# Row-sum reciprocals on GpSimd, and the score banks as two tiles, in a fused top-k attention and feed-forward kernel

## The chip, the core and the metric

The kernel runs on one core of a Trainium2 chip. The time is device microseconds of one execution. The engines are called as in the profile: PE (TensorE matmul), PEld (its weight loads), DVE (VectorE), ACT (ScalarE), POOL (GpSimd) and SP (SyncE, which only issues DMAs here). Each engine works through its own queue in order and waits on semaphores for the others.

## The reference

Eight batches of eight heads, 576 tokens, head size 64. Each query keeps its 32 highest scores, takes a softmax over them and sums the values; the result, 4608 rows of 512, goes through a feed-forward block with an ELU of width 2048.

```python
scores = scale * np.matmul(q, k.transpose(0, 1, 3, 2))
kth = np.partition(scores, -top_k, axis=-1)[..., -top_k:-top_k + 1]
scores = np.where(scores >= kth, scores, -1000000000.0)
scores = scores - np.max(scores, axis=-1, keepdims=True)
attn = np.exp(scores)
attn = attn / (np.sum(attn, axis=-1, keepdims=True) + 1e-09)
attn_out = np.matmul(attn, v)
x = attn_out.transpose(0, 2, 1, 3).reshape(B * S, H * D)
h = x @ w_in
g = np.where(h > 0.0, h, np.exp(np.minimum(h, 0.0)) - 1.0)
out = g @ w_out
```

## The kernel before

The work is cut into 144 steps. A step is one tile of 128 queries and a pair of heads, so two rows of scores per partition (row 0 and row 1), each 576 wide. The steps overlap: while step n is in its selection, step n+2 gets its scores, step n-1 its mask and exponentials, and step n-2 its transposes.

`scores` (L289) writes four matmul results (L298) into PSUM: `wide` is one tile of four banks, banks 0 and 1 for the two halves of row 0, banks 2 and 3 for row 1; each half takes 288 of a bank's 512 columns. Two ACT instructions (L306) copy them to SBUF as `sc`. The free columns behind them serve as well: `transpose_qk` (L246) puts the last keys and queries of a head pair through bank 1 (L256, read by ACT at L261), and `turn` (L385) puts the fifth of nine transposed score chunks through bank 3 (L400 with output `scps`, read by ACT at L401). The other chunks go through a pool of their own (L400 with output `eps`), as do the other transposes of keys and queries (L268, read by ACT at L274).

`select` (L332) finds the 32nd highest value with four passes of MAX8 (L339, L351) and three of MATCH_REPLACE8 (L344) on DVE, both rows in turn. `select_row` (L311; L317, L321, L327) does the same in the first eight steps. `mask` (L355) has POOL negate that value and form a difference (L364, L366), and ACT runs Prelu and Exp over the row in place (L367, L368), with the sums of the row in `den`. `normalise` (L372) adds epsilon on POOL (L377), takes the reciprocal on DVE (L379) and scales both rows on POOL (L381). `attend` (L410) multiplies the transposed chunks with the values (L426), and ACT copies the result into `xT` (L453).

The feed-forward block is cut into pieces. `hidden` has 4 matmuls (L484), three ACT instructions (L496 to L498) and later one on DVE (L465); `project` has matmuls (L507), whose results ACT copies (L516) for the store. `feed` slips these pieces between the parts of the steps, by costs and due times fixed in the source. The weights come as raw 64-bit numbers and are decoded during the first eight steps on ACT (L167 to L169), POOL (L170, L184) and DVE (L177, L180).

In these eight steps a scheduler orders the instructions of each engine. From the ninth on (`n == tight`, L657) the four compute engines keep the order of the source. In a step of this kind `mask` of the rows of the step before comes in the first half, and `normalise` after the last selection pass of the current step:

```python
        next(passes)
        if prev:
            normalise(prev)
        feed(n, 0.25)
        turn_qk(True)
```

Of the kernel before, what the change touches and what calls it, by code (L numbers as in the profile page):

```python
# [8 lines left out]
AF = mybir.ActivationFunctionType  # L9
ALU = mybir.AluOpType  # L10
FP32 = mybir.dt.float32
# [69 lines left out]
def kernel(  # L81
# [9 lines left out]
    nc = tc.nc  # L91
    P = nc.NUM_PARTITIONS
# [3 lines left out]
    JP = J * P  # L96
    R = S - JP
    HS = S // 2
# [6 lines left out]
    scale = 1.0 / float(D) ** 0.5  # L105
# [3 lines left out]
    def pool(name, bufs, **kw):  # L109
        return ctx.enter_context(tc.tile_pool(name=name, bufs=bufs, **kw))  # L110

    const = pool("const", 1)
# [8 lines left out]
    ps_sc = pool("ps_sc", 1, space=PSUM)  # L121
    ps_t = pool("ps_t", 2, space=PSUM)
    ps_f = pool("ps_f", 2, space=PSUM)
    wide = ps_sc.tile([P, 4, JP], FP32, tag="s", name="scps")
    late = {}
    raws = ExitStack()
    early = raws.enter_context(tc.tile_pool(name="early", bufs=1))
# [2 lines left out]

    ident = const.tile([P, P], FP32, tag="ident", name="ident")
    make_identity(nc, ident[:])
    w_in = const.tile([P, NC, dff], FP32, tag="w_in", name="w_in")
    w_out = const.tile([P, NF, dm], FP32, tag="w_out", name="w_out")

# [110 lines left out]
    def transpose_qk(b, hp):  # L246

        d = kvpool.tile([P, 4 * J + 3, D], FP32, tag="kqT", name="kqT")
        kqT[b, hp] = d[:].rearrange("p c d -> p (c d)")
        srcs = [loaded.pop((b, hp, name)) for name in ("k", "q")]
        ps = wide[:, 1, HS : HS + 3 * R]
        for i in range(2):
            nc.tensor.transpose(  # L256
                ps[:, i * R : i * R + P],
                srcs[0][:, J, :, :].rearrange("p h d -> p (h d)"),
                ident[:],
            )  # L260
        nc.scalar.copy(  # L261
            d[:, 0 : 4 * J + 3 : 2 * J + 1, :],
            ps.rearrange("p (a s) -> p a s", a=3),
        )
        for i, src in enumerate(srcs):
            ps = ps_t.tile([P, JP], FP32, tag="t", name="qkps")
            for c in range(J):
                nc.tensor.transpose(  # L268
                    ps[:, c * P : (c + 1) * P],
                    src[:, c, :, :].rearrange("p h d -> p (h d)"),  # L270
                    ident[:],
                )
            c0 = KEYS + i * (2 * J + 1) * D
            nc.scalar.copy(kqT[b, hp][:, c0 : c0 + JP], ps[:])  # L274
            yield

    def start_qk(b, hp):
        turning.append(transpose_qk(b, hp))
# [10 lines left out]
    def scores(u):  # L289

        u.sc = scpool.tile([P, 2, S], FP32, tag="sc", name="sc")
        q0 = QUERIES + u.t.qt * P
        for half in range(2):
            for h, i, rows in u.heads:
                kq = kqT[u.t.b, h // 2]
                part = slice(i * D, (i + 1) * D)
                k0 = (KEYS if i == 0 else 0) + half * HS
                nc.tensor.matmul(  # L298
                    wide[rows, 2 * i + half, 0:HS],
                    kq[part, q0 : q0 + u.t.ql],  # L300
                    kq[part, k0 : k0 + HS],
                    start=True,
                    stop=True,
                )
        for i in range(2):
            nc.scalar.activation(  # L306
                u.sc[:, i, :].rearrange("p (a s) -> p a s", a=2),
                wide[:, 2 * i : 2 * i + 2, 0:HS], AF.Copy, scale=scale,
            )

    def select_row(u, i):  # L311
# [58 lines left out]
        )  # L370

    def normalise(u):  # L372
        if u.normal:
            return
        u.normal = True
        den = small.tile([P, 2], FP32, tag="dene", name="dene")
        nc.gpsimd.tensor_scalar_add(den[:], u.den[:], EPS)  # L377
        rec = small.tile([P, 2], FP32, tag="rec", name="rec")
        nc.vector.reciprocal(rec[:], den[:])  # L379
        for i in range(2):  # L380
            nc.gpsimd.tensor_scalar(  # L381
                u.sc[:, i, :], u.sc[:, i, :], rec[:, i : i + 1], 1.0, ALU.mult, ALU.mult
            )

    def turn(u, chunks):  # L385

        if u.turned:
            return
        g = u.group
        if g.et is None:  # L390
            g.et = etpool.tile([P, 2 * J + 1, len(g.tiles), P], FP32, tag="et", name="et")
        if chunks.stop - chunks.start == 1:
            ps = wide[:, 3, HS : HS + P]
        else:
            ps = ps_t.tile([P, JP], FP32, tag="t", name="eps")
        sc = u.sc[:, :, :].rearrange("p i s -> p (i s)")
        n = chunks.stop - chunks.start
        for c in range(n):
            c0 = (chunks.start + c) * P
            nc.tensor.transpose(ps[:, c * P : (c + 1) * P], sc[:, c0 : c0 + P], ident[:])  # L400
        nc.scalar.copy(  # L401
            g.et[:, chunks, u.at, :],
            ps[:, 0 : n * P].rearrange("p (c q) -> p c q", c=n),
        )
        if chunks.stop == 2 * J + 1:
            u.turned = True
            if u.at == len(g.tiles) - 1:
                closing.append(g)
# [127 lines left out]
    for b in range(B):  # L536
# [12 lines left out]
        for qt in range(J + 1):  # L549
            r0 = b * S + (JP if qt == J else qt)  # L550
            if qt == J:
                (blk, slot), c0, n = slots[rest], (b % 2) * R, R
                rows = slice(r0, r0 + R)
            else:
                (blk, slot), c0, n = slots[(b % 2) * J + qt], 0, P
                rows = slice(r0, r0 + J * (P - 1) + 1, J)
# [26 lines left out]
    for b in range(1, B):  # L583
        f = first[b]
# [30 lines left out]
    start_qk(0, 0)  # L615
    turn_qk(True)
    scores(steps[0])
    load_qk(0, 2)
    start_qk(0, 1)
    turn_qk(True)  # L620
    scores(steps[1])
    load_qk(0, 3)
    for hp in range(1, NHP):
# [10 lines left out]
    for n in range(NS + 3):  # L634
# [3 lines left out]
        if n < tight:  # L638
            turn_qk(True)
            scores(ahead)  # L640
            for i in range(2):
                passes = select_row(cur, i)
                next(passes)
                if i == 0:
                    while closing:
                        attend(closing.pop(0))
                elif prev:
                    normalise(prev)
                    turn(prev, main)
                    turn(prev, rest)  # L650
                    turn(prev, other)
                feed(n, 0.25)
                next(passes)
                mask(cur, i)
                feed(n, 0.25)
            continue
# [27 lines left out]
        if prev:  # L684
            normalise(prev)
# [38 lines left out]
```

## Time and profile before

| | |
|---|---|
| time, median of 3 runs | 1712.81 us (1712.72 to 1713.59) |
| time of the profiled execution | 1713.55 us |
| its span, first to last instruction | 1711.8 us |
| PE, PEld busy | 93%, 60% |
| DVE, ACT, POOL busy | 91%, 69%, 25% |
| mean granted TensorE clock | 0.973 |
| HBM traffic over the span | 32 GB/s |

A line of the profile names the source line, the engine, the operation, and the tiles written and read ("rec<-dene"). "Idle before" is time for which the engine stood still in front of an instruction, with the instruction that ended the wait. Matmuls overlap, and so do instructions that follow each other closely on one engine, so starts are a better measure of an engine's pace than durations. In a timeline the columns are the start, the time and the count of a merged run of equal instructions.

### The profile page before, as it was taken

What the parts mean: (1) busy time and instruction counts of PE and PEld (TensorE: products, weight loads), DVE (VectorE), ACT (ScalarE), POOL (GpSimd) and SP (SyncE); (2) the same over time, 40 slices, a digit from 0 to 9 for tenths busy, and PEclk for the clock granted to TensorE, in tenths of its full rate; (3) what the DMA queues carried; (4) which work ended last, traced back from release to release, by engine and by line L of the source; (5) the groups of instructions that cost most, each with busy time, mean ns of one, the idle gap of its engine ahead of it and who ended that gap; (6) DMA issues with size and microseconds to landing.
All of it is one profiled execution on the core that took longest, in us unless ns stands there. A gap on an engine that the chain in (4) does not pass through costs nothing.

```text
span 1711.8 us, 26507 instructions
## 1 busy us (share of the span) xinstructions
PE 1593.9 (93%) x8560; PEld 1029.6 (60%) x8560; DVE 1551.1 (91%) x3392; ACT 1180.3 (69%) x2813; POOL 432.7 (25%) x1142
## 2 busy tenths in 40 slices
PE   4558999999999999999999999999999999999999
PEld 3345676667575666655557575755557575755565
DVE  7899999999999999999999999999989999998600
ACT  5886786778686776768658585867758686767531
POOL 3664222222222222222222222222222212222100
PEclk8569999999999999999999999999999999999999
DMA  6531021001100111001100111001100000000000
GB/s 168 171 126 54 15 48 35 7 7 43 48 7 7 29 35 41 1 15 41 43 18 1 34 35 35 7 13 40 32 26 7 21 21 28 7 7 7 7 13 13
DMA packets 101130, 56.24 MB, mean 33 GB/s; under 512 B 84096, under 2 KB 92288, under 8 KB 100992
## 3 DMA queue, kind: packets, MB, share of 16 engines
q1 hardware_dynamic: 100992, 54.55, 11.5%
q8 instruction: 68, 1.11, 0.3%
q14 instruction: 70, 0.57, 0.1%
HBM read 45.09 MB, written 9.44 MB: 32 GB/s over the span
## 4 chain that ended last, share of the span: by engine, by line
PE 64%; DVE 23%; ACT 8%; issue 3%; POOL 1%; DMA 1%; SPq 0%; ACTq 0%; POOLq 0%
PE ops L507 25%; PE hps L484 19%; DVE wk L344 8%; PE avps L426 7%; DVE m L351 7%; PE scps L298 6%; PE eps L400 4%; DVE m L339 2%; DVE gT L465 2%; ACT sc L367 2%; ACT sc L368 2%; DVE wk L321 1%; DVE m L327 1%; ACT et L401 1%; ACT n L498 1%
## 5 line engine op out<-in xcount | busy, mean ns | idle before, releaser
L484 PE MATMUL hps<-xT,w_in 128*128 128x256 f32 (+2 forms) x2432 | 555.7, 377 | 24.8 <-ACT gT L497 16.9
L351 DVE MAX8 m<-wk 128x8 f32<-128x576 f32 x816 | 574.9, 745 | 0.0
L507 PE MATMUL ops<-w_out,gT 128*128 128x512 f32 x1152 | 522.6, 598 | 0.0
L484 PEld LDWEIGHTS hps<-xT,w_in 128*128 128x128 f32 x2432 | 410.1, 194 | 126.0 <-ACT gT L497 23.8
L344 DVE MATCH_REPLACE8 wk<-m,wk 128x576 f32<-128x576 f32 x544 | 399.5, 741 | 0.0
L507 PEld LDWEIGHTS ops<-w_out,gT 128*128 128x128 f32 x1152 | 208.6, 190 | 232.8 <-issue 197.5
L381 POOL TENSOR_SCALAR sc<-sc,rec 128x576 f32<-128x576 f32 x288 | 218.8, 769 | 254.7 <-DVE rec L379 234.0
L367 ACT ACTIVATE sc<-sc,neg 128x576 f32<-128x576 f32 x288 | 226.6, 787 | 55.9 <-POOL neg L364 55.6
L377 POOL TENSOR_SCALAR dene<-den 128x2 f32<-128x2 f32 x144 | 34.4, 239 | 879.5 <-ACT sc L368 878.9
L368 ACT ACTIVATE sc<-sc,gap 128x576 f32<-128x576 f32 x288 | 223.2, 775 | 26.3 <-ACT sc L367 1.5
L306 ACT ACTIVATE sc<-scps 128x576 f32<-128x576 f32 x288 | 173.0, 660 | 80.5 <-PE scps L298 80.4
L401 ACT COPY et<-eps 128x512 f32<-128x512 f32 x288 | 167.2, 581 | 74.3 <-PE eps L400 74.2
L426 PE MATMUL avps<-et,vT 128*64 128x256 f32 (+2 forms) x2080 | 190.4, 324 | 14.3 <-ACT et L401 13.7
L400 PE MATMUL eps<-ident,sc 128*128 128x128 f32 x1152 | 177.8, 280 | 24.7 <-POOL sc L381 24.6
L400 PEld LDWEIGHTS eps<-ident,sc 128*128 128x128 f32 x1152 | 145.2, 145 | 92.2 <-issue 48.4
L344 DVE MATCH_REPLACE8 wk<-m,sc 128x576 f32<-128x576 f32 x272 | 199.7, 741 | 0.0
L298 PE MATMUL scps<-kqT 64*128 64x288 f32 (+1 forms) x1280 | 186.5, 440 | 11.1 <-ACT et L401 6.1
L339 DVE MAX8 m<-sc 128x8 f32<-128x576 f32 x272 | 191.2, 744 | 0.0
L496 ACT ACTIVATE n<-hps 128x256 f32<-128x256 f32 (+2 forms) x304 | 112.4, 370 | 91.9 <-PE hps L484 89.0
L465 DVE SCALAR_TENSOR_TENSOR gT<-n,gT 128x256 f32<-128x256 f32 (+2 forms) x304 | 128.9, 430 | 49.6 <-ACT n L498 49.6
L426 PEld LDWEIGHTS avps<-et,vT 128*64 128x64 f32 x2080 | 120.6, 140 | 87.8 <-issue 28.7
L298 PEld LDWEIGHTS scps<-kqT 64*128 64x128 f32 (+1 forms) x1280 | 100.2, 182 | 76.6 <-issue 22.2
(43 smaller groups left out, 1066.1 us busy)
## 6 DMA issues: line engine op xcount, KB each, us to landing
kin<-in_k_dram SPq DMA_DIRECT2D x64, 128.0 KB, 2.8
qin<-in_q_dram SPq DMA_DIRECT2D x64, 128.0 KB, 2.8
raw<-in_moe_w_in_dram SPq DMA_DIRECT2D x16, 512.0 KB, 4.1
vT<-in_v_dram SPq DMA_DIRECT2D x64, 128.0 KB, 2.2
raw<-in_moe_w_out_dram SPq DMA_DIRECT2D x16, 512.0 KB, 3.2
out_dram<-osb SPq DMA_DIRECT2D x32, 256.0 KB, 2.2
kin<-in_k_dram SPq DMA_DIRECT2D x32, 32.0 KB, 2.5
kin<-in_q_dram SPq DMA_DIRECT2D x32, 32.0 KB, 2.3
```

The lines of the kernel that those rows point to most:

```text
L298: nc.tensor.matmul(wide[rows, 2 * i + half, 0:HS], kq[part, q0 : q0 + u.t.ql], kq[part, k0 : k0 + HS], start=True, stop=True,)
L339: nc.vector.max(found[i], cur[i])
L344: nc.vector.match_replace(wk[i], found[i], cur[i], TAKEN)
L351: nc.vector.max(found[i], cur[i])
L367: nc.scalar.activation(sc, sc, AF.Prelu, bias=neg[:], alpha=STEEP)
L368: nc.scalar.activation(sc, sc, AF.Exp, bias=gap[:], accum_out=u.den[:, i : i + 1])
L381: nc.gpsimd.tensor_scalar(u.sc[:, i, :], u.sc[:, i, :], rec[:, i : i + 1], 1.0, ALU.mult, ALU.mult)
L400: nc.tensor.transpose(ps[:, c * P : (c + 1) * P], sc[:, c0 : c0 + P], ident[:])
L401: nc.scalar.copy(g.et[:, chunks, u.at, :], ps[:, 0 : n * P].rearrange("p (c q) -> p c q", c=n),)
L426: nc.tensor.matmul(ps[i * D : (i + 1) * D, cols], vt[:, 2 * J + i if c == J else i * J + c, :], w, start=(c == 0), stop=(c == J),)
L484: nc.tensor.matmul(ps[:, 0:n_tok], w_in[:, i, f * P : (f + 1) * P], blk.xT[:, i, 0:n_tok], start=(i == 0), stop=(i == NC - 1),)
L507: nc.tensor.matmul(blk.o[:], blk.gT[f // NG][:, f % NG, s * P : (s + 1) * P], w_out[:, f, :], start=(f == 0), stop=(f == NF - 1),)
```

## The change

DVE's reciprocal becomes four instructions on POOL: the sum to the power of -1 (with a constant tile `power` as the exponent), and a Newton step r(2 - dr) in three instructions, all on 128 x 2 numbers. The epsilon add before them and the scaling behind them stay on POOL. The constant tile takes one POOL memset at the start. The score tile of four banks becomes two tiles of two banks, one for each row; every use is renamed to the same bank as before, so the columns and the order in the source stay as they were.

```diff
-    wide = ps_sc.tile([P, 4, JP], FP32, tag="s", name="scps")
+    wide = [ps_sc.tile([P, 2, JP], FP32, tag=f"s{i}", name="scps") for i in range(2)]
...
+    power = const.tile([P, 2], FP32, tag="power", name="power")
+    nc.gpsimd.memset(power[:], -1.0)
...
-        ps = wide[:, 1, HS : HS + 3 * R]
+        ps = wide[0][:, 1, HS : HS + 3 * R]
...
-                    wide[rows, 2 * i + half, 0:HS],
+                    wide[i][rows, half, 0:HS],
...
-                wide[:, 2 * i : 2 * i + 2, 0:HS], AF.Copy, scale=scale,
+                wide[i][:, :, 0:HS], AF.Copy, scale=scale,
...
         rec = small.tile([P, 2], FP32, tag="rec", name="rec")
-        nc.vector.reciprocal(rec[:], den[:])
+        nc.gpsimd.tensor_tensor(rec[:], den[:], power[:], ALU.pow)
+        nc.gpsimd.tensor_tensor(den[:], den[:], rec[:], ALU.mult)
+        nc.gpsimd.tensor_scalar(den[:], den[:], -1.0, 2.0, ALU.mult, ALU.add)
+        nc.gpsimd.tensor_tensor(rec[:], rec[:], den[:], ALU.mult)
...
-            ps = wide[:, 3, HS : HS + P]
+            ps = wide[1][:, 1, HS : HS + P]
```

## The prediction, made before the changed kernel ran

> **What bounds the kernel now.** I read the page first (busy shares and the 40 slices), then a table of stages, then the waits of PE and of DVE by stage, and last a timeline of one step.
>
> ```profile
> span 1711.8 us, 26507 instructions
> PE 1593.9 (93%) x8560; PEld 1029.6 (60%) x8560; DVE 1551.1 (91%) x3392; ACT 1180.3 (69%) x2813; POOL 432.7 (25%) x1142
> ```
>
> Two engines are nearly full, so the average says little. The table of stages (busy time of PE, PEld, DVE, ACT, POOL in each stretch, then granted clock, DMA share and GB/s) separates them.
>
> ```profile
> 0.00:150.00 150.00, 83.29 (x457) 62.66 (x459) 127.67 (x249) 112.40 (x251) 85.66 (x130) 0.72 0.49 146
> 150.00:800.00 650.00, 614.63 (x3695) 410.84 (x3691) 643.13 (x1439) 472.20 (x1182) 155.80 (x455) 1.00 0.10 25
> 800.00:1640.00 840.00, 828.23 (x4180) 513.97 (x4177) 773.51 (x1691) 577.60 (x1330) 191.23 (x558) 1.00 0.08 21
> 1640.00:1712.00 72.00, 67.73 (x238) 42.10 (x236) 6.80 (x16) 18.12 (x53) 0.00 (x0) 1.00 0.03 11
> ```
>
> From 150 to 800 us DVE is busy 643.1 of 650 and PE idles 35.4: DVE is the bound. From 800 to 1640 PE is busy 828.2 of 840 and DVE idles 66: PE is the bound, with 11.8 us of holes. After 1640 only PE's feed-forward matmuls are left. The opening holds eight steps and the decoding of the weights.
>
> PE's waits, first from 150 to 800 (two of its rows), then all of 800 to 1640, then DVE's waits for the reciprocal's input in those two stretches (us in total, times, longest):
>
> ```profile
> PE scps L256 <- ACT sc L306: 8.5, 6, 1.9
> PE scps L400 <- ACT kqT L261: 5.4, 6, 1.5
> ```
>
> ```profile
> PE scps L400 <- ACT kqT L261: 8.0, 8, 2.2
> PE scps L256 <- ACT sc L306: 3.2, 2, 1.9
> PE avps L426 <- ACT et L401: 0.2, 1, 0.2
> ```
>
> ```profile
> DVE rec L379 <- POOL dene L377: 6.5, 7, 1.6
> ```
>
> ```profile
> DVE rec L379 <- POOL dene L377: 51.9, 26, 14.3
> ```
>
> Nearly all of PE's holes after 800 stand in front of writes to the score banks. L400 (the fifth transpose, bank 3) waits for L261, which reads bank 1: another bank, so the wait comes from the banks being one tile. The timeline of one step shows the chain of the row sums:
>
> ```profile
> 511.88 0.23 POOL L377 TENSOR_SCALAR dene<-den 128x2 f32<-128x2 f32 x1 [4.51 <-ACT sc L368]
> 514.09 1.41 DVE L351 MAX8 m<-wk 128x8 f32<-128x576 f32 x2
> 515.41 0.15 DVE L379 RECIPROCAL rec<-dene 128x2 f32<-128x2 f32 x1
> 515.48 0.40 DVE L465 SCALAR_TENSOR_TENSOR gT<-n,gT 128x256 f32<-128x256 f32 x1
> 515.73 1.49 POOL L381 TENSOR_SCALAR sc<-sc,rec 128x576 f32<-128x576 f32 x2 [3.62 <-DVE rec L379]
> 516.78 0.57 PEld L400 LDWEIGHTS eps<-ident,sc 128*128 128x128 f32 x4
> 517.19 0.42 POOL L364 TENSOR_SCALAR neg<-m 128x1 f32<-128x1 f32 x1
> 517.64 0.78 ACT L367 ACTIVATE sc<-sc,neg 128x576 f32<-128x576 f32 x1 [1.21 <-POOL neg L364]
> ```
>
> The sum plus epsilon is ready at 512.11. POOL then idles 3.62 us, until DVE has worked off its queue and comes to the reciprocal; POOL scales the rows only then, and the negated threshold of the next rows (L364) stands behind that, with ACT waiting 1.21 us for it.
>
> **Part 1: the reciprocal leaves DVE.** 144 RECIPROCALs, 0.151 us each, are 21.8 us of busy time. But DVE's instructions overlap: here the next one starts 0.07 us after the reciprocal, and without it would start where the reciprocal did. So the queue gains about 0.065 us a step: 62 steps from 150 to 800, 4.0 us. The wait for L377 goes too: 6.5 us there. That is 10.5 us at most where DVE is the bound. PE has 35.4 us of holes in the stretch, so it can follow, but where DVE waited, ACT or PE were late themselves. I take 7. After 800 the 51.9 us of DVE waits are worth nothing by themselves, since PE is busy 98.6%: DVE would only wait elsewhere, for scores. Its instruction order on the long part of the run is otherwise unchanged in the built program.
>
> **Part 2: four instructions more on POOL.** The chain from L377 to L381 becomes power, multiply, multiply-add, multiply, each waiting for the one before. Multiply: 0.19 us (TENSOR_TENSOR L366, 53.7 us over 288). Multiply-add: 0.23 (L377). A hand-over within an engine: about 0.1 us (ACT's L367 to L368). No row shows a power. From below it is the 0.19 of L366; the longest TENSOR_TENSOR that the trace has on POOL, L184's 1.28 us for 512 columns, is the other end. I take 0.5, nearer the lower row because there are only two columns. Chain: 0.5 + 0.19 + 0.23 + 0.19 + five hand-overs of 0.1 = 1.6 us (1.3 to 2.4), in place of a mean 1.6 us that POOL waits for DVE now (234.0 us over 144) and 0.3 for the hand-overs there and back.
>
> What hides it: in the step shown PE takes the scaled rows at 516.78 and one scaling lasts 0.75, so it may begin as late as 516.03, that is 3.9 us after L377's end. Over the steps from the ninth on the same subtraction gives 3.0 at the least, 3.5 for one in twenty, 5.9 in the middle. So up to 3 us this chain costs nothing, and mostly L381 and the neg behind it come earlier, which takes part of ACT's 55.6 us of waiting for neg. Queued behind the chain on POOL are L381, then L364 and L366 of the next rows; ACT's L367 waits for those.
>
> The Trainium skill speaks against the move: GPSIMD Engine Reference, section 4.1 Engine selection, calls GpSimd about twice as slow as VectorE on two-input elementwise work. At one or two columns the rows say 0.187 against 0.151. By the rule the three two-input instructions would take 0.30 each and the chain 1.6 us, still under the cover, so the sum would not change.
>
> **Contention.** L465 reads two SBUF tiles; it usually takes 0.40 us at 256 columns, 0.423 in the mean, once 1.28 (the longest of any form). The excess of that form is 176 x 0.023 = 4.0 us. POOL gets 144 x 1.1 = 160 us busier on 433, so a third more: 1 to 3 us over the run, half of it where DVE binds. It is in the step from 10.5 to 7. The skill's page SBUF — State Buffer, section Who interferes with whom, gives the reason: a DVE instruction with two SBUF inputs fetches the second through the read interface shared with GpSimd. By the rule alone, if each added POOL instruction held up one of DVE's for its whole length, 160 us would go; the row, where 433 us of POOL work cost 4, is far below that.
>
> **Part 3: two score tiles.** In the built program L400's wait for L261 is gone (it now waits for the second eviction L306, which is earlier), L256 waits for the first of the two evictions (one eviction, 0.65 us, sooner), and the first score matmul L298 waits for nothing, with the second taking over the wait for L401. ACT's first eviction starts one matmul sooner. After 800: 8.0 us of L261 waits plus 2 x 0.65 = 9.3; what comes next, the transposes that wait for L274's copy, stands behind four or more matmuls. I take 9. Before 800 the same waits (5.4 us and part of 8.5) lie beside a full DVE and only give PE room.
>
> **Part 4: opening and tail.** The scheduler orders the opening anew on all engines. DVE waits 21.9 us there for POOL's L170, and POOL gets 7 x 1.1 = 8 us more work in a stretch where it is 57% busy; the reciprocals' wait is gone in return. Between -4 and +10; I take +1. The tail is PE's alone: 0.
>
> **Sum.** -7 - 9 + 1 = -15 us. The profiled execution took 1713.55 (span 1711.8 and 1.75 around it), 0.74 above the median of 1712.81: 1698.5 on it, 1698 as a median.
>
> **Rivals.**
> Slower: power is a long software loop. POOL's cycle is neg at 517.19, through ACT's four passes, to the next L377's end at 522.82: 5.6 us, then the chain, then 1.5 of scaling; 7.1 + chain. Steps take 10.8 us (L339 from 144.0 to 1606.0 over 135 steps). From a chain of 3.7 us, a power of about 2.6, POOL is the bound, and each further us costs 136: a power of 3 us gives some 1750, of 4 us some 1890. For: no row has it. Against: two columns only.
> No change: ACT and PE's own lateness holds DVE up elsewhere, PE meets the next wait (L274, gT) after each one removed, and the opening loses 8: -15 becomes -3 to +3, 1710 to 1716. For: both engines are nearly full, so relief on one is soon capped by the other.
> Slower by the opening alone: POOL's added 8 us and the new order land on DVE's L177 in full, and part 1 gives 2, part 3 gives 3: +5, 1718.
> The change does not do what it says: excluded for the waits, which the built program shows; the gain of part 3 could still be a shift.
>
> **The numbers.** 0.2% (3.4 us) is about what a measurement can tell. My forecast 0.64, own range 1685 to 1708 (all of 10.5, 11.8, and 4 to 6 from the opening and earlier ACT work below; 2 + 5 less 2 above). No change 0.12; long power 0.17; opening 0.07. Faster 0.64, same 0.12, slower 0.24. The range 1685 to 1718 leaves out the long power and little else.
>
> **What would show it.** Right: no L379 on DVE and no waits there; L400 no longer waiting for L261; PE over 99% busy from 800; L381 starting 1.3 to 2.4 us after L377's end. Wrong: a power over 2.6 us, ACT waiting longer for neg than 55.6 us, PE's eps waiting for POOL after 150 us, or an opening that ends later (first L339 after 144.0).

## The result, and the profile after

The changed kernel takes 1694.03 us (median of 4 runs, 1692.54 to 1695.23) against 1713.07 (4 runs): ratio 0.9888, 95% interval 0.9877 to 0.9900. That is 19 us faster; 15 had been forecast. The profiled execution has a span of 1693.4 us against 1711.8.

The page of the changed kernel (span; busy time, share and instructions):

```profile
span 1693.4 us, 26805 instructions
PE 1597.5 (94%) x8560; PEld 1035.0 (61%) x8560; DVE 1542.7 (91%) x3248; ACT 1179.6 (70%) x2813; POOL 627.0 (37%) x1719
```

The stages (stretch; PE, PEld, DVE, ACT, POOL busy; clock; DMA; GB/s), the last one now ending at 1694:

```profile
0.00:150.00 150.00, 88.73 (x435) 64.93 (x437) 124.04 (x231) 108.52 (x240) 90.52 (x155) 0.72 0.50 146
150.00:800.00 650.00, 621.97 (x3738) 417.59 (x3737) 649.97 (x1399) 477.75 (x1196) 244.28 (x714) 1.00 0.10 25
800.00:1640.00 840.00, 837.24 (x4225) 521.22 (x4224) 762.77 (x1606) 579.09 (x1337) 292.24 (x851) 1.00 0.08 21
1640.00:1694.00 54.00, 49.52 (x167) 31.23 (x165) 5.96 (x14) 14.29 (x44) 0.00 (x0) 0.99 0.03 10
```

From 150 to 800 us DVE no longer stands still at all (650.0 of 650), and from 800 to 1640 PE's holes shrink from 11.8 to 2.8 us. PE's waits from 800 to 1640 after the change, all of them:

```profile
PE scps L258 <- ACT sc L308: 2.1, 2, 1.3
PE avps L432 <- ACT et L407: 0.2, 1, 0.2
```

The 8.0 us in front of the fifth transpose (now L406) are gone, as the split into two tiles promised. DVE's waits in that stretch are not fewer, they only have another name:

```profile
DVE gT L471 <- ACT n L504: 76.6, 21, 42.9
```

The row-sum chain in one step, by the timeline (start, time):

```profile
500.77 0.23 POOL L380 TENSOR_SCALAR dene<-den 128x2 f32<-128x2 f32 x1 [4.58 <-ACT sc L370]
501.08 0.72 POOL L382 TENSOR_TENSOR rec<-dene,power 128x2 f32<-128x2 f32 x1
501.88 0.21 POOL L383 TENSOR_TENSOR dene<-dene,rec 128x2 f32<-128x2 f32 x1
502.17 0.19 POOL L384 TENSOR_SCALAR dene<-dene 128x2 f32<-128x2 f32 x1
502.45 0.20 POOL L385 TENSOR_TENSOR rec<-rec,dene 128x2 f32<-128x2 f32 x1
502.75 1.48 POOL L387 TENSOR_SCALAR sc<-sc,rec 128x576 f32<-128x576 f32 x2
504.25 0.23 POOL L366 TENSOR_SCALAR neg<-m 128x1 f32<-128x1 f32 x1
```

From the end of L380 (501.00) to the scaling (502.75) it is 1.75 us; over the steps 1.73 in the middle. POOL no longer idles in it. The next rows' neg follows 0.02 us behind the scaling; in this step its input, a MAX8 of L353, was done only 0.07 us before the scaling's end (504.16 against 504.23). How tight this place is, the experiments e5 to e8 ask.

Two of the prediction's own signs of being wrong did come: the opening ends later (the first MAX8 of the ninth step at 150.3 instead of 144.0 us), and ACT's waits for neg are 56.1 us against 55.6, though part of them had been expected to go.

**Where the time went.** PE's order of instructions is the same in both kernels after the opening, so the start of the same matmul in two traces tells how far one is ahead. Negative is earlier than in the kernel before, in us. "Ninth step" is the first MAX8 of the ninth step on DVE (144.0 us before), the others are feed-forward matmuls of L484, the 129th, 1153rd and 2049th of them, which started at 169.0, 760.7 and 1463.3.

| run | ninth step, DVE | PE at 169 | PE at 761 | PE at 1463 | end |
|---|---|---|---|---|---|
| the change | +6.3 | +1.9 | -4.7 | -18.3 | -18.4 |
| e1, tiles only | +1.7 | +1.0 | -4.2 | -18.4 | -18.4 |
| e2, reciprocal only | +6.5 | +0.4 | -5.6 | -5.7 | -5.6 |
| e3, change, DVE reciprocal in the opening | +2.2 | +3.5 | -7.4 | -21.6 | -21.6 |
| e4, change, idle reciprocal on DVE | +5.7 | +1.3 | -3.4 | -17.1 | -17.1 |
| e5, two powers more | +16.5 | +13.3 | +15.6 | +16.0 | +18.5 |
| e6, four powers more | +26.3 | +26.4 | +85.9 | +138.9 | +148.8 |
| e7, no Newton step | +9.3 | +2.4 | -8.7 | -23.0 | -23.0 |
| e8, e7 and idle POOL work | +9.3 | +2.4 | -8.5 | -22.8 | -22.8 |
| e9, a version from these | +2.1 | +3.2 | -8.8 | -23.1 | -23.1 |
| e10, e9 without the Newton step | +2.0 | +3.1 | -7.9 | -22.2 | -22.2 |
| e11, the change again | +6.7 | +2.3 | -5.0 | -18.7 | -18.7 |

So the change lost 1.9 us in the opening as PE sees it, gained 6.6 between 169 and 761, and 13.6 after that. Each row is one execution. The two of the changed kernel agree within 0.4 us, but the executions of one kernel spread over 1 to 4 us, and the profiled one is the slowest of four for the change and the fastest of four for e1; a difference of 1 or 2 us between two rows shows little.

### The profile page after: what moved, and what is told of

Read it like the earlier page. It is cut to its first block, busy times and chain, and to the rows that moved or that the text cites. A ratio compares the mean times of both kernels' runs of the same rounds, so it can differ in the third digit from the quotient of the medians.

```text
span 1693.4 us, 26805 instructions
## 1 busy us (share of the span) xinstructions
PE 1597.5 (94%) x8560; PEld 1035.0 (61%) x8560; DVE 1542.7 (91%) x3248; ACT 1179.6 (70%) x2813; POOL 627.0 (37%) x1719
## 4 chain that ended last, share of the span: by engine, by line
PE 68%; DVE 21%; ACT 5%; issue 2%; POOL 2%; DMA 1%; SPq 0%; ACTq 0%; POOLq 0%; DVEq 0%
PE ops L513 25%; PE hps L490 21%; PE avps L432 8%; DVE wk L346 7%; PE scps L300 7%; DVE m L353 6%; PE eps L406 5%; DVE m L341 2%; DVE gT L471 1%; DVE wk L323 1%; DVE m L329 1%; PE qkps L270 1%; ACT sc L370 1%; ACT sc L369 1%; ACT et L407 1%
## 5 line engine op out<-in xcount | busy, mean ns | idle before, releaser
L353 DVE MAX8 m<-wk 128x8 f32<-128x576 f32 x816 | 574.9, 745 | 0.0
L490 PE MATMUL hps<-xT,w_in 128*128 128x256 f32 (+2 forms) x2432 | 554.3, 376 | 19.3 <-ACT gT L503 19.3
L490 PEld LDWEIGHTS hps<-xT,w_in 128*128 128x128 f32 x2432 | 409.5, 194 | 119.9 <-ACT gT L503 26.4
L380 POOL TENSOR_SCALAR dene<-den 128x2 f32<-128x2 f32 x144 | 34.9, 243 | 819.6 <-ACT sc L370 819.0
L369 ACT ACTIVATE sc<-sc,neg 128x576 f32<-128x576 f32 x288 | 226.5, 787 | 56.6 <-POOL neg L366 56.1
L387 POOL TENSOR_SCALAR sc<-sc,rec 128x576 f32<-128x576 f32 x288 | 218.7, 769 | 15.2 <-POOL rec L385 0.4
L300 PE MATMUL scps<-kqT 64*128 64x288 f32 (+1 forms) x1280 | 198.1, 438 | 21.5 <-ACT sc L308 14.7
L471 DVE SCALAR_TENSOR_TENSOR gT<-n,gT 128x256 f32<-128x256 f32 (+2 forms) x304 | 129.1, 431 | 95.3 <-ACT n L504 95.3
L406 PEld LDWEIGHTS eps<-ident,sc 128*128 128x128 f32 x1152 | 144.5, 145 | 93.4 <-issue 48.9
L406 PE MATMUL eps<-ident,sc 128*128 128x128 f32 x1152 | 177.9, 280 | 21.8 <-POOL sc L387 18.6
L300 PEld LDWEIGHTS scps<-kqT 64*128 64x128 f32 (+1 forms) x1280 | 106.0, 180 | 90.2 <-issue 45.1
```

The costliest lines, as they stand in the source:

```text
L300: nc.tensor.matmul(wide[i][rows, half, 0:HS], kq[part, q0 : q0 + u.t.ql], kq[part, k0 : k0 + HS], start=True, stop=True,)
L353: nc.vector.max(found[i], cur[i])
L369: nc.scalar.activation(sc, sc, AF.Prelu, bias=neg[:], alpha=STEEP)
L387: nc.gpsimd.tensor_scalar(u.sc[:, i, :], u.sc[:, i, :], rec[:, i : i + 1], 1.0, ALU.mult, ALU.mult)
L490: nc.tensor.matmul(ps[:, 0:n_tok], w_in[:, i, f * P : (f + 1) * P], blk.xT[:, i, 0:n_tok], start=(i == 0), stop=(i == NC - 1),)
```

## The experiments

**e1 and e2: each part alone.** e1 makes the two tiles of the change and keeps DVE's reciprocal; e2 does the reverse.

```diff
 e1: + wide = [ps_sc.tile([P, 2, JP], ...) for i in range(2)]   (and its four uses)
       nc.vector.reciprocal(rec[:], den[:])
 e2:   wide = ps_sc.tile([P, 4, JP], ...)
     + power, tensor_tensor(pow), mult, mult-add, mult on nc.gpsimd
```

> Only the two score tiles; the reciprocal stays on DVE. The split theory (both parts pay: the reciprocal where DVE binds, the tiles where PE binds): PE's holes in front of L400 and L256 go after 800 us, -9 to -13 us there, before 800 DVE still waits for the reciprocal's input and little is gained (0 to -3); opening 0; in all about -11, 1702. The tiles-alone theory (PE's instruction order is the clock everywhere, and all of the gain stood in front of the banks): -18 to -24, 1689 to 1695, the whole gain of the change or more.

> Only the reciprocal on GpSimd; one score tile as before. Split theory: -7 between 150 and 800 us, nothing after it, since PE still waits for L261 in front of L400 (some 8 us after 800), and +2 to +6 in the opening; in all -3 to -7, about 1708. Tiles-alone theory: 0 in the long part and the opening's loss, 1713 to 1718.

e1: 1696.74 us, ratio 0.9899 (0.9886 to 0.9913). e2: 1707.90, 0.9967 (0.9954 to 0.9979). The gains, 16.8 and 5.6 us against 1713.53 in the same job, add up to 22.4, and both together give 19. (By the medians alone this difference of 3.4 us is hardly clear of the noise: each of the three gains is good to about 2 us.) Neither theory is right as stated. The tiles pay in both stretches (-5.2 between 169 and 761, -14.2 after), the reciprocal in the first alone (-6.0, then -0.1). Together they give -6.6 in the first stretch, not -11.2. Part of the overlap is seen in the wait of DVE for the sum from 150 to 800 us, which was 6.5 us before; with the tiles alone it is

```profile
DVE rec L379 <- POOL dene L377: 2.6, 4, 0.8
```

Freeing PE fills holes of DVE, and so does letting DVE go on without the sum; it can only be done once. In that stretch DVE stands still for 6.9 us before, 2.6 in e1, 2.6 in e2 and not at all in the change: each part alone takes 4.3, both together 6.9. That is 1.7 of the 4.6 us by which the parts fall short of their sum; where the rest goes isn't shown. After 800 us e2 shows the wait that only the tiles remove still in place:

```profile
PE scps L405 <- ACT kqT L263: 7.7, 6, 2.2
```

On top of the tiles, the reciprocal's move is worth 2 to 3 us by the medians (1696.74 against 1694.03 and, in e11, 1694.72) and nothing by the profiled executions (-18.4 both); the intervals of the ratios overlap.

**e3: the opening.**

```diff
-                    normalise(prev)           # in the steps before the ninth
+                    normalise(prev, True)     # True: nc.vector.reciprocal
```

> The change, but the first eight steps (those that the scheduler orders) keep the reciprocal on DVE. If GpSimd's extra work there is what makes the opening later, the ninth step starts near 144 us again and PE's first feed-forward matmuls are 2 to 3 us earlier: 1688 to 1692. If the opening's loss comes from the new order that the two tiles give, it stays: 1693 to 1695.

1692.36 us, ratio 0.9873 (0.9860 to 0.9887), 2 us below the change by the medians, with intervals that overlap. The ninth step starts at +2.2 instead of +6.3. PE's landmark at 169 us is not earlier (+3.5), but the gain is there at 761 (-7.4 against -4.7). Four of the 6.3 us come from the reciprocal's move, 1.7 from the order that the tiles give (e1). That it is POOL's added work is not shown: e7 below has less of it in the opening (POOL busy 85.4 us up to 150 against 90.5), and its ninth step starts later still (+9.3). The scheduler orders the opening anew in each of these kernels, and that may be all of it.

**e4: the place in DVE's queue.**

```diff
+        idle = small.tile([P, 2], FP32, tag="idle", name="idle")
+        nc.vector.reciprocal(idle[:], power[:])
```

> The change, with a reciprocal of a constant on DVE at the old place in each step, which waits for nothing and which nobody reads. If the reciprocal's place in DVE's queue is what costs where DVE binds (0.065 us a step), +4 between 150 and 800 us: 1697 to 1699. If it is the wait for the sum that cost, or PE alone sets the pace, 0 to +1: 1694 to 1695.

1696.19 us, ratio 0.9898 (0.9883 to 0.9913), 2.2 us over the change's first median. From the ninth to the 71st step on DVE (144.0 to 799.3 us before) the trace goes from +5.7 to -1.7, the change's from +6.3 to -4.9: 3.8 us for 62 steps, 0.06 each, near the 0.065 read from the starts; against e11's trace it is 2.6, 0.04 each. At the end 1.3 of them are left (-17.1 against -18.4). A little issue time on the bound engine is real, and most of it no longer shows where PE binds.

**e5 and e6: is the chain under cover?** Two and four powers more, each waiting for the one before.

```diff
         nc.gpsimd.tensor_tensor(rec[:], den[:], power[:], ALU.pow)
+        for _ in range(2):                     # e6: 4
+            nc.gpsimd.tensor_tensor(rec[:], rec[:], power[:], ALU.pow)
```

> The change with two more powers in the chain (1/x twice, so the value comes back): the time from the sum plus epsilon to the scaling grows from 1.73 to about 3.3 us in every step. Cover theory (PE takes the scaled rows 3 us or more after the sum in every step, 5.9 in the middle): 0 to +4 us, 1694 to 1698, half of it in the opening. Loop theory (POOL, ACT's four passes and POOL again make a cycle of 5.7 + chain + 1.5, against a step of 10.6): the cycle is 10.5, just under the step, so also little, up to +5.

> The change with four more powers: chain about 4.9 us. Loop theory: the cycle is 5.7 + 4.9 + 1.5 = 12.1 against 10.6 a step, so POOL becomes the bound and the steps lengthen by 1.5 each, +150 to +210 us, 1850 to 1900. Cover theory alone (only steps whose scaling comes later than PE needs it pay): a few tens at most, 1700 to 1730.

e5: 1731.65 us, ratio 1.0106 (1.0090 to 1.0123), with a chain of 3.28 us in the middle. e6: 1866.70, 1.0889 (1.0872 to 1.0906), chain 4.81. The cover theory falls: e5 costs 37 us where 0 to 4 were expected, 11 of them in the opening (+13.3 against +1.9 at 169) and the rest along the whole run. Nor is it for want of the scaled rows: PE waits for them (L408) 6.5 us in e5 from 150 to 1640. The loop theory missed e5 too (up to +5), since it took a cycle of 10.5 against a step of 10.6 for room enough. e6 is what it said. The loop can be read from e6's timeline:

```profile
500.72 1.48 POOL L389 TENSOR_SCALAR sc<-sc,rec 128x576 f32<-128x576 f32 x2
...
502.17 0.24 POOL L366 TENSOR_SCALAR neg<-m 128x1 f32<-128x1 f32 x1
...
502.44 0.78 ACT L369 ACTIVATE sc<-sc,neg 128x576 f32<-128x576 f32 x1 [0.65 <-POOL neg L366]
...
506.53 0.23 POOL L380 TENSOR_SCALAR dene<-den 128x2 f32<-128x2 f32 x1 [3.65 <-ACT sc L370]
506.84 0.72 POOL L382 TENSOR_TENSOR rec<-dene,power 128x2 f32<-128x2 f32 x1
507.64 2.99 POOL L384 TENSOR_TENSOR rec<-rec,power 128x2 f32<-128x2 f32 x4
...
511.57 1.48 POOL L389 TENSOR_SCALAR sc<-sc,rec 128x576 f32<-128x576 f32 x2
```

Scaling, neg, ACT's four passes, the sum, the chain, the next scaling: 500.72 to 511.57, 10.85 us with ACT at its quickest (502.17 to 506.76, 4.59). Over the steps ACT's part is 5.3 us in the middle: 5.3 + 4.8 + 1.5 = 11.6, and the steps last 11.6 us up to the 71st and 11.8 after. In e5 the same sum is 5.6 + 3.3 + 1.5 = 10.4, or 11.0 with ACT's 6.2 in the later half, and the steps last 10.5 and 11.1. This agreement is no proof by itself: where neg starts directly behind the scaling (115 of 136 steps in e5 and in e6) the sum comes to about a step, whichever engine binds. That the loop binds is seen in ACT, which takes neg up 0.04 us after its end in the middle of e5 and 0.03 in e6, against 0.81 in the change; its part shrinks from 6.9 us to 5.7 and 5.3. Its waits for neg over the run, first the change, then e5, then e6, say the same:

```profile
ACT sc L369 <- POOL neg L366: 56.1, 46, 3.3
```

```profile
ACT sc L369 <- POOL neg L366: 153.4, 86, 6.5
```

```profile
ACT sc L369 <- POOL neg L366: 326.9, 123, 7.3
```

In the change neg starts directly behind the scaling in 92 of 136 steps (115 before), but ACT mostly has other work when neg is ready, so the loop isn't tight there. What looked like cover is this other work of ACT, which fits into the loop while there is room; the two powers of e5 use the room up.

**e7 and e8: shorter chain, or less work on POOL?** e7 leaves out the Newton step, so its reciprocals have the power's own precision. e8 does too, and puts three idle multiplies of constants where POOL waits for the exponentials.

```diff
 e7: -  nc.gpsimd.tensor_tensor(den[:], den[:], rec[:], ALU.mult)
     -  nc.gpsimd.tensor_scalar(den[:], den[:], -1.0, 2.0, ALU.mult, ALU.add)
     -  nc.gpsimd.tensor_tensor(rec[:], rec[:], den[:], ALU.mult)
 e8: +  if i == 1 and ordered:              # in mask, from the ninth step on
     +      for _ in range(3):
     +          idle = small.tile([P, 2], FP32, tag="idle", name="idle")
     +          nc.gpsimd.tensor_tensor(idle[:], power[:], power[:], ALU.mult)
```

> The change without the Newton step (the power's own precision): three POOL instructions fewer in each step, chain about 0.9 us. If the chain is under cover, nothing in the long part, and 0 to -2 from POOL's lighter opening: 1692 to 1694. If POOL's extra instructions cost DVE or ACT something all along, -3 or more.

> The power alone (no Newton step), and from the ninth step on three POOL multiplies of constants that nobody reads, put where POOL waits for the exponentials, so POOL does the same amount of work as in the changed kernel but the chain stays at 0.9 us. Chain theory (what counts is the time from the sum to the next rows' neg): as without the Newton step, 1690 to 1692. Work theory (POOL's extra instructions hold others up wherever they stand): as the changed kernel, 1693 to 1695.

e7: 1691.42 us, ratio 0.9872 (0.9857 to 0.9887). e8: 1691.32, 0.9871 (0.9857 to 0.9886). A chain of 0.9 instead of 1.73 us gives 3 us, and the same work outside the chain costs nothing: it is not POOL's load that counts. That it is the length of the loop is not shown. The gain comes before 761 us (-8.7 against -4.7), and from the ninth to the 71st step DVE doesn't stand still in either kernel, so what e7 gains there must lie in DVE's own work. In large part it does: from the start of a two-input instruction (L471 in the change) to the start of the next takes 38.5 us in sum in e7 and e8, 41.7 in the change and 42.9 in e11, and most of the difference is time for which POOL's scaling holds these instructions up (1.1 and 1.2 us against 3.7 and 4.9; more on this under contention below). With the shorter chain the scaling falls beside fewer of them; no run separates this from the loop. e11, the changed kernel again in the job of e8, ran at 1694.72, ratio 0.9891 (0.9876 to 0.9906).

> The changed kernel once more, on the same chip as these three, as their measure: 1692 to 1696 by every theory.

**e9 and e10: a better version.** Two tiles, DVE's reciprocal in the first eight steps, GpSimd's after them, and no epsilon add; e10 leaves out the Newton step as well.

```diff
-        nc.gpsimd.tensor_scalar_add(den[:], u.den[:], EPS)
...
+        if early:
+            nc.vector.reciprocal(rec[:], u.den[:])
+        else:
+            nc.gpsimd.tensor_tensor(rec[:], u.den[:], power[:], ALU.pow)
+            ...                                # e9: the Newton step on u.den
```

> A version that the runs point to: two score tiles, DVE's reciprocal in the first eight steps, GpSimd's power and Newton step after them, and no epsilon add (the sum holds exp(0) = 1, beside which 1e-9 vanishes in fp32), so the chain is one instruction shorter, about 1.45 us. By chain theory -1 against the change with DVE's reciprocal in the opening: 1689 to 1692. If the chain is well under cover: 1692.

> The same without the Newton step (the power's own precision): chain about 0.6 us. By chain theory another -2 to -3: 1686 to 1690. If the chain is well under cover: 1692.

e9: 1688.56 us, ratio 0.9857 (0.9843 to 0.9872), 6 us below the change in the same job. e10: 1689.38, 0.9856 (0.9840 to 0.9873). e9 is just below what was expected; e10 lies inside its range of 1686 to 1690, but its further 2 to 3 us below e9 did not come, and the runs of the two overlap. So a chain shorter than about 1.45 us shows no gain in this version. What binds there was not tried; in the trace of e9 PE still waits 14.3 us for ACT's reading of PSUM into gT (L504 there, L497 before) between 150 and 800 us.

## Why the prediction was right, and which steps were wrong

The sign, the size (-15 against -19) and the two places were right. The sum, -7 - 9 + 1, had three terms that were off and partly cancelled; the traces give -6.6, -13.6 and +1.9. That the total came out so near is luck in part: the tiles alone give 16.8 us where 9 had been put on them, and the reciprocal on top of them 2 to 3 where 7 had been.

- **Part 1, 7 us where DVE binds.** Alone it was 6.0 (e2). The step that failed is the sum over the parts, which took them as separate. Part 3 was put at nothing before 800 us, "beside a full DVE". It gave 5.2 there (e1). DVE's waits for the sum were in part PE's lateness handed on: they fall from 6.5 to 2.6 us with the tiles alone. After that only 1.4 of part 1 was left. The reading that DVE's 51.9 us of waits after 800 were worth nothing held: e2 gains 0.1 there.
- **Part 3, 9 us after 800.** The waits named were the right ones, the term was too small: 14.2 alone. Compared start by start, the fifth transpose is 9.8 us earlier in sum, L256 1.1, and matmuls of L484 that follow each other 2.8. The wait table gave 8.0 for the first, probably because the modelled end of a matmul covers the beginning of a wait. The third stands in no wait table: in the kernel before, PE's granted clock was half of full speed for 3.4 us (0.50 from 817.80 to 821.20) right behind two of the longest holes, and the eight matmuls of L484 behind the fifth transpose took 4.29 us there; the same eight take 2.75 in the change, where the hole is gone (before, then change):

  ```profile
  817.89 0.45 PE L400 MATMUL scps<-ident,sc 128*128 128x128 f32 x1 [2.20 <-ACT kqT L261]
  818.13 4.29 PE L484 MATMUL hps<-xT,w_in 128*128 128x384 f32 x8
  ```

  ```profile
  810.33 0.27 PE L406 MATMUL scps<-ident,sc 128*128 128x128 f32 x1
  810.44 2.75 PE L490 MATMUL hps<-xT,w_in 128*128 128x384 f32 x8
  ```

  The other place is at 1183.0 us, behind a wait of 1.86 us at L256 (1.32 in the change, and no such stretch behind it). The 2.2 us of hole in front of 1211.8 are not followed by one. In these traces the clock changes only at the ends of windows of 3.41 us (817.8 and 1183.0 are 107 of them apart); the first two holes lie in one window each, the third is cut in two by an end at 1210.35, which may be why, but no run tests it. In the change and in e1 no such stretch is left between 800 and 1640 us.
- **Part 2, the chain.** 1.6 us forecast, 1.73 measured. The power was taken as 0.5 and is 0.72 us, within the ends of 0.19 and 1.28; a hand-over costs 0.08. The step that failed is "up to 3 us this chain costs nothing". That came from the moment at which PE takes the scaled rows. The nearer deadline was neg, behind the scaling on POOL (e5 and e6). So 3.3 us cost 37 (e5). A chain 0.8 us shorter than the change's gave 3 (e7), but for another reason, at least in part (contention, below). The slower rival had the right mechanism, and its threshold of 3.7 was too high: it set one step's ACT time of 5.6 us against the mean step of 10.8. By e5's ACT times and the change's steps it would be 10.4 - 5.6 - 1.5 = 3.3 up to the 71st step and 10.8 - 6.2 - 1.5 = 3.1 after it. Each further us cost 88 from e5 to e6, not 136, as ACT's part shrank. The change's chain stayed below either threshold.
- **Contention, 1 to 3 us.** DVE's two-input instruction took 128.9 us in all before and 129.1 after, with 194 us more of POOL's busy time: no net cost. But the two engines do collide. A two-input instruction of DVE that begins while a pass of POOL's scaling runs is longer than usual by what the pass has left, less 0.14 us. Here the second pass began at 523.11, had 0.62 us left, and made an instruction of usually 0.40 us one of 0.89:

  ```profile
  522.38 1.48 POOL L387 TENSOR_SCALAR sc<-sc,rec 128x576 f32<-128x576 f32 x2
  523.24 0.89 DVE L471 SCALAR_TENSOR_TENSOR gT<-n,gT 128x256 f32<-128x256 f32 x1
  ```

  That happened 23 times before (4.9 us in sum), 18 times in the change (4.8), 44 in e5 (12.0), 14 in e7 (4.3). The added instructions hold up nothing: 41 of the L471 began beside the row-sum chain, 23 of them during a power, and none was more than 0.06 us longer than usual. So what counts is where POOL's long passes fall, and not how much it does, as the estimate took it.
- **The opening, +1.** +6.3 on DVE and +1.9 on PE: mis-sized, inside the ends given. e3 puts about 4 of the 6.3 on the reciprocal's move; whether by POOL's work or by the new order is open.
- **The rivals.** No change needed the next wait to take each gain back. That came near to true for part 1 on top of part 3, and not for part 3 itself.

## What to carry to other kernels

When two engines are both nearly full, waits of the one are often lateness of the other handed on: two edits that fill the same hole don't add up, so run each alone. A hole can cost more than its length: behind two of them the clock was half for 3.4 us here. A small chain on a lightly used engine is not free because that engine is idle; follow the loop through every engine that its in-order queue feeds, and take the earliest deadline, not the most visible one. And one PSUM tile for several banks ties unrelated writes together: a wait between different columns of one tile is worth looking for.

## What was not expected of the hardware

A power on GpSimd over 128 x 2 numbers takes 0.72 us, almost always the same:

```profile
L382 POOL TENSOR_TENSOR rec<-dene,power x144: 718/719/997, 28.9 to 1611.9; 128x2 f32<-128x2 f32 x144
```

That is near four times a multiply of the same shape (0.195), and in a waiting chain the next instruction starts 0.77 to 0.80 us after a power's start and 0.28 after a multiply's (e5, e6).
